# Sparse attention and a two-layer network on one core: GpSimd's casts of batch 1 ahead of its memsets, mask comparison and loads of batch 2

## The chip, the core and the metric

The kernel runs on one core of a Trainium2 chip. The core has five engines that run side by side, each through its own list of instructions in order: TensorE (PE; its weight loads are shown apart as PEld), VectorE (DVE), ScalarE (ACT), GpSimd (POOL) and SyncE (SP), which here only starts transfers. The metric is the device time of one execution in microseconds (us), as the median of several runs. An engine waits for another through semaphores, and a waiting instruction holds up everything behind it on its engine.

## What is computed

The reference first computes attention with two kinds of sparse mask, and then a two-layer network with a leaky activation on its output:

```python
scores = scale * np.matmul(q, k.transpose(0, 1, 3, 2))        # 8 batches, 8 heads, 576 positions, 64 wide
mask_local = (rel >= 0) & (rel < stride)                      # heads 0 to 3, stride 32
mask_strided = (rel >= 0) & (pos[None, :] % stride == pos[:, None] % stride)   # heads 4 to 7
scores = np.where(masks[None, :, :, :], scores, -1000000000.0)
attn = exp(scores - max) / (sum + 1e-09)
x = (attn @ v), heads side by side                            # 4608 rows of 512
h = x @ w_in                                                  # 512 to 2048
g = np.maximum(h, 0.0) + alpha * np.minimum(h, 0.0)
out = g @ w_out                                               # 2048 to 512
```

q, k, v and the weights arrive as float32; the kernel multiplies in float16.

## The kernel before, in words

A batch has four pairs of heads: pairs 0 and 1 of a batch are local (queries in blocks of 96), pairs 2 and 3 strided (blocks of 72). So pairs 4 to 7 are batch 1, and a "unit" is the local or the strided half of a batch: unit 2 is batch 1 local, unit 3 batch 1 strided, unit 4 batch 2 local. The network works on chunks of 512 rows, nine in all.

Each pair goes through the same steps. `load_qk` (L126) brings q and k in as float32 for the local halves (tiles `ql`, `kl`), the strided halves of later batches already as float16. `cast_l` (through `cast_copy`, L213 on ScalarE, L215 on VectorE, L217 on GpSimd) turns the local ones to float16. `transpose_piece` (L280) turns blocks of q and k on TensorE into PSUM, and ScalarE or VectorE copies them to `qT` and `kT`; `tails` does the same for the last 64 positions. `score_early` (L334) or `score_both` (L450) multiplies q and k, ScalarE takes the exponentials into one of six `et` tiles, and a multiplication by the 0/1 mask `mmul` follows, on VectorE (L355) in the early pairs and on GpSimd (L470, L477) later. `pv_piece` (L512) multiplies by v, in two or three groups of blocks; VectorE divides by the row sum (L521, L523). `x_piece` (L533) turns the result into `xT`, the input of the network. The transposes, the products with v and `x_piece` share three PSUM buffers, so a new one has to wait until an earlier one has been copied out.

A chunk's first layer is 16 pieces of four matmuls (`lin1_piece`, L678), each followed by ScalarE (`neg`, L697) and VectorE (`gT`, L700). The second layer of chunk 0 is 16 pieces of four matmuls (`lin2_piece`, L715); every fourth of a row block ends in a copy (L720) and a store (L721) from SyncE. Chunks from 1 on use a scheme with seven products in place of eight for 2 x 2 blocks, with sums of weights (`w_sums`, L748, VectorE) and of `gT` (`g_sum`, L760).

All instructions keep the order in which the program writes them (`keep`). The order around the change is written by hand as lists of tokens that `run` works off. List `first` (L949) does batch 0's attention. Then the rest of the weights and batch 1 are loaded from GpSimd (L968 to L970), the loop at L978 computes the first layer of chunk 0, and the list at L999 weaves batch 1's attention into chunk 0's second layer: `("M", i)` is a piece of the second layer, `("T", u, "q")` transposes of unit u, `("t", u)` its tails, `("C", 1, "q", 0, "pool")` the cast of one half of batch 1's local q on GpSimd, `("V", ...)` a copy of v, `("S", g)` the scores of pair g, `("K", g)` its masks, `("P", g, i)` group i of its product with v, `("X", g)` its `x_piece`, `("O", ...)` a copy of the overlap of v's blocks, and `("I", fn, ...)` any other call.

Before the change GpSimd does three things late in the first layer and early in the second (L984 to L987 and L1000 to L1004): it sets columns 640 to 800 of the six `et` tiles to zero (L986; VectorE sets 576 to 640 at the start, L912), it makes `mmul` by a comparison of the additive mask (L987), and it issues the loads of batch 2's local q and k (L126), tails (L187) and v (L205), partly ahead of the two casts of batch 1 (L217). A piece that is not part of attention of batch 1, the deferred exponentials, concerns later chunks: `score_both` puts some of its exponentials off (`defer`), and `pv_piece` (L488) runs those that it needs before it starts.

Of the kernel before, what the change touches and what calls it, by code (L numbers as in the profile page):

```python
# [11 lines left out]
ALU = mybir.AluOpType  # L12
# [20 lines left out]
def kernel(  # L33
# [10 lines left out]
    nc = tc.nc  # L44
    keep = tc.keep_in_program_order
# [27 lines left out]
    mmul = cpool.tile([128, 360], F16)  # L73
    madd = consts[:, 128:488]
# [27 lines left out]
    ets = [cpool.tile([128, 800], F16, name=f"et{i}") for i in range(NE)]  # L102
# [7 lines left out]
    def load_qk(b, strided, nm):  # L110

        h0 = 4 if strided else 0
        src = q if nm == "q" else k
        if strided and b:
            t16 = hpool.tile([128, 2, 512], F16, tag=f"{nm}s", bufs=2, name=f"{nm}s")
            cast16[(b, True, nm)] = t16
        else:
            t16 = hpool.tile([128, 2, 512], F32, tag=f"{nm}l", bufs=2, name=f"{nm}l")  # L120
            loaded[(b, strided, nm)] = t16
        base = src[b, h0 : h0 + 1, 0:1, :]
        eng = nc.sync if (b > 2 and not strided) or (b == 0 and strided) else nc.gpsimd
        if b == 0 and strided and nm == "q":
            eng = nc.scalar
        keep(eng.dma_start(t16, bass.AP(  # L126
            tensor=base.tensor, offset=base.offset,
            ap=[[8 * D, 64], [2 * S * D, 2], [S * D, 2], [1, 8 * D]])))
# [41 lines left out]
    def cast_l(b, nm, eng="pool", ts=(0, 8)):  # L170
        if (b, False, nm) not in cast16:
            cast16[(b, False, nm)] = hpool.tile(
                [128, 8, 2, 64], F16, tag=f"{nm}l16", bufs=2, name=f"{nm}l16")
        t16 = cast16[(b, False, nm)]
        src = loaded[(b, False, nm)].rearrange("p f (t d) -> p t f d", t=8)
        cast_copy(eng, t16[:, ts[0] : ts[1]], src[:, ts[0] : ts[1]])
# [42 lines left out]
    def cast_v(b, pr, eng):  # L219

        v16 = vss[b % 2]
        cast_copy(eng, v16[0:72, 2 * pr : 2 * pr + 2, :, 0:64],
                  loaded[b][0:72, 1024 * pr : 1024 * pr + 1024].rearrange(
                      "p (h t d) -> p h t d", h=2, t=8))
        cast16[(b, True, "v")] = v16
# [133 lines left out]
    def run_masks(P=None):  # L359

        for z in list(dmask):
            z[0] += P is None
            if z[0] > 1 or z[1] is P:
                z[2]()
                dmask.remove(z)
# [57 lines left out]
    defer, defer_et = [], {}  # L423
# [61 lines left out]

    def pv_piece(P, a):
        run_masks(P)
        while defer and any(P.et[z][0] is defer_et["et"] for z in P.et):  # L488
            defer.pop(0)()
        if P.x16 is None:  # L490
            if P.xd and P.strided:
                P.x16 = x16s
            else:
                P.x16 = xpool.tile([128, 1024], F16, tag="x16", name="x16")
        raw = P.strided and P.b == 0
        v16 = None if raw else cast16[(P.b, P.strided, "v")]
        grp = P.pgroups[a]
        r = 72 if P.strided else 128
        pv = pspool.tile([128, 512], F32, tag="ps", name="pv")
        nb = 2 * len(grp)  # L500
        for x in range(nb):
            t, hh = grp[x // 2], x % 2
            et, c = P.et[(t, hh)]
            if raw:
                d0 = 512 * (2 * P.pr + hh) + 64 * t
                for o, rhs in ((pv[:, 65 * x : 65 * x + 64], loaded[0][0:r, d0 : d0 + 64]),
                               (pv[:, 65 * x + 64 : 65 * x + 65], vss[0][0:r, 0, 0, 64:65])):
                    keep(nc.tensor.matmul(
                        o, et[0:r, c : c + 128], rhs, start=(x == 0 and o.shape[1] == 64),
                        stop=(x == nb - 1 and o.shape[1] == 1), skip_group_check=True))  # L510
                continue
            keep(nc.tensor.matmul(  # L512
                pv[:, 65 * x : 65 * x + 65], et[0:r, c : c + 128],
                v16[0:r, 2 * P.pr + hh, t, :] if P.strided else v16[:, 6 * (2 * P.pr + hh) + t, :],
                start=(x == 0), stop=(x == nb - 1), skip_group_check=True))
        while late:
            late.pop(0)()
        w = P.w
        rc = rpool.tile([128, 8], F32, tag="rc", name="rc")
        pvv = pv[0:w, 0 : 65 * nb].rearrange("r (c e) -> r c e", e=65)  # L520
        keep(nc.vector.reciprocal(rc[0:w, 0:nb], pvv[:, :, 64]))  # L521
        c0 = 128 * grp[0]
        keep(nc.vector.tensor_tensor(  # L523
            P.x16[0:w, c0 : c0 + 64 * nb].rearrange("r (c e) -> r c e", e=64),
            pvv[:, :, 0:64],
            rc[0:w, 0:nb].unsqueeze(2).to_broadcast([w, nb, 64]), op=ALU.mult))
# [16 lines left out]
    def x_dma(P):  # L543
        base = (P.b % 4) * S
        if P.strided:
            P.xs = xpool.tile([128, 8, 80], F16, tag="xs", bufs=2, name="xs")
            keep(nc.sync.dma_start_transpose(P.xs, P.x16[0:80, :]))
        else:
            keep(nc.sync.dma_start_transpose(
                xT[:, P.hp, base : base + S].rearrange("r (w p) -> r w p", p=96), P.x16[0:96, 0:768]))  # L550
# [26 lines left out]
    for g in range(7, npair + 2):  # L577
        c = g // 4
        a, p, t = g, g - 1, g + 1
# [28 lines left out]
        for i, (kind, fn) in enumerate(seq):  # L608
# [6 lines left out]
            def run(fn=fn, extra=extra, g=g, c=c, kind=kind, lastp=(i == lastP), first=(i == 0), i_last=(i == len(seq) - 1)):  # L615
                fn()
                for b, pr in extra:
                    if pr in ("q", "k"):
                        if b < LX:
                            cast_l(b, pr, "act" if b == 3 else "pool")  # L620
                        if b + 1 < LX:
                            load_qk(b + 1, False, pr)
                        continue
                    cast_v(b, pr, "pool")
                    if pr == 1 and b > 2 and b + 1 < B:
                        load_v(b + 1, True)
                if kind == "Tk" and g % 4 == 3 and c + 3 < LX:
                    load_tail(c + 3, False)
                if lastp:
                    if 4 * DX <= g - 1 < npair and pairs[g - 1].xd:  # L630
                        x_dma(pairs[g - 1])
                    if g % 4 == 3 and DX <= c + 1 < B:
                        transpose_d()
                    if g % 4 == 2 and DX <= c and c + 1 < B:
                        load_d(c + 1)
                    if g % 4 == 1 and DX < c and c + 1 < B:
                        load_v(c + 1, False)
                if first and g % 4 == 2 and LX <= c + 1 < B:
                    transpose_l(c + 1)
                if i_last and g % 4 == 3 and LX <= c + 2 < B:  # L640
                    for nm in "qk":
                        load_l(c + 2, nm)
                if first and 4 * DX <= g - 3 < npair and pairs[g - 3].xd and pairs[g - 3].strided:
                    x_copy(pairs[g - 3])
# [264 lines left out]
        keep(nc.vector.memset(kTs[i][:, :, 0:32], 0.0))  # L909
        keep(nc.vector.memset(kTs[i][:, :, 608:672], 0.0))  # L910
    for t in ets:
        keep(nc.vector.memset(t[:, 576:640], 0.0))  # L912
    load_tail(0, False)
    load_v(0, True)
    load_v(0, False)
# [13 lines left out]
    def w_next(*which):  # L929
        for z in which:  # L930
            load_w(*z)
# [33 lines left out]
                late.pop(0)()  # L965

    run(first)
    w_next((2, True), (3, True))  # L968
    load_unit(1, True)
    load_unit(1, False)  # L970
# [7 lines left out]
    for m in (2, 1, 0, *range(3, 16)):  # L978
        if m in (3, 4):
            banks.append(pspool.tile([128, 512], F32, tag="ps", name="hx"))  # L980
            turn.insert(0, m)
        lin1_piece(0, m)
        attn_n(0, 0)
        if m == 6:  # L984
            for t in ets:
                keep(nc.gpsimd.memset(t[:, 640:800], 0.0))  # L986
            keep(nc.gpsimd.tensor_scalar(mmul, madd, -1.0, 1.0, op0=ALU.is_ge, op1=ALU.mult))  # L987
    for z in (3, 4):
        turn.remove(z)
    do.update({  # L990
# [6 lines left out]
        "I": lambda fn, *a: fn(*a),  # L997
    })
    run([  # L999
        ("M", 0), ("M", 4), ("I", load_qk, 2, False, "q"), ("I", load_qk, 2, False, "k"),  # L1000
        ("C", 1, "q", 0, "pool"), ("I", w_sums, nc.vector, (1,)), ("M", 5), ("M", 6),
        ("I", load_tail, 2, False), ("M", 1), ("I", w_sums, nc.vector, (2,)), ("T", 3, "q"),
        ("M", 2), ("T", 3, "k"), ("I", w_sums, nc.vector, (4,)), ("V", 1, 0, "dve"),
        ("I", load_v, 2, False), ("t", 3), ("M", 7), ("C", 1, "k", 1, "pool"), ("M", 3),  # L1004
        ("V", 1, 1, "dve"), ("S", 6), ("M", 8), ("C", 1, "q", 1, "dve"), ("K", 6),
        ("C", 1, "k", 0, "dve"), ("T", 2, "q"), ("P", 6, 0), ("S", 7), ("P", 6, 1), ("M", 9),
        ("T", 2, "k"), ("t", 2), ("M", 10), ("K", 7), ("P", 6, 2), ("S", 5), ("P", 7, 0), ("M", 11),
# [68 lines left out]
```

## Time and profile before

| | before |
|---|---|
| three runs, us | 300.86, 299.57, 301.13 (median 300.86) |
| profiled execution | 300.0 us, span 298.1 us |
| TensorE clock granted | 1.00 |
| busy share VectorE, ScalarE, GpSimd | 76%, 58%, 57% |
| read from and written to memory | 38.60 MB, 9.44 MB |

The page gives for one execution the busy time of each engine, the span in slices, the transfers, the chain of work that ended last, and the costliest groups of instructions. In a row of the timeline the columns are start in us, duration in us, engine, line of the kernel, operation, tiles as output<-inputs, shape and count; in brackets stands how long the engine had been idle before it, and what released it. Matmuls are pipelined and their ends are modelled, so starts say more than ends. DMA-issuing instructions of GpSimd appear with the time that the issue took; the landing of a transfer is given apart.

### The profile page before, as it was taken

How to read it: one execution, taken by the hardware profiler on the slowest of the kernel's cores; microseconds unless marked ns; L12 is line 12 of the kernel's file. 1: busy time of each engine (PE TensorE's matmuls, PEld its weight loads, DVE VectorE, ACT ScalarE, POOL GpSimd, SP SyncE). 2: the span in 40 equal slices, each digit the busy share in tenths (PEclk: the TensorE clock that was granted, in tenths of full speed). 3: DMA queues.
4: the chain of work that ended last, by engine and by line, in shares of the span. 5: the costliest groups of instructions: out<-in, count | busy, mean ns of one | idle time of the engine just before them, and what ended most of it. 6: DMA issues, size and time to landing. Idle time of an engine off the chain costs nothing.

```text
span 298.1 us, 7107 instructions
## 1 busy us (share of the span) xinstructions
PE 289.9 (97%) x2808; PEld 193.6 (65%) x2808; DVE 227.8 (76%) x427; ACT 173.5 (58%) x325; POOL 168.5 (57%) x182
## 2 busy tenths in 40 slices
PE   7899998999999999999999999999999999999995
PEld 3664445644886478646898887468746864784584
DVE  5788868979975988488848894889488858946872
ACT  3566556888557773776377636763676257406620
POOL 8952289359757996777777778665555003101300
PEclk9999999999999999999999999999999999999999
DMA  7999999995998969999999999993811140022004
GB/s 219 204 202 207 205 238 266 170 175 178 177 154 186 111 100 127 173 192 160 132 209 177 138 141 182 184 144 54 201 22 21 24 141 0 2 71 73 0 2 141
DMA packets 102273, 41.01 MB, mean 138 GB/s; under 512 B 80720, under 2 KB 99424, under 8 KB 102240
## 3 DMA queue, kind: packets, MB, share of 16 engines
q0 software_dynamic: 56336, 19.25, 61.1%
q1 hardware_dynamic: 45632, 20.78, 35.3%
q10 hardware_dynamic: 272, 0.52, 0.6%
q8 instruction: 22, 0.36, 0.6%
q14 instruction: 11, 0.09, 0.1%
HBM read 38.60 MB, written 9.44 MB: 161 GB/s over the span
## 4 chain that ended last, share of the span: by engine, by line
PE 80%; DMA 11%; POOL 4%; issue 2%; DVE 2%; ACT 1%; POOLq 0%
PE hb L678 36%; PE hb L811 32%; DMA ks<-in_k_dram 6%; PE pv L512 4%; DMA win<-in_moe_w_in_dram 3%; PE sp L450 2%; DMA ql<-in_q_dram 2%; PE hb L715 2%; PE opl L811 1%; PE xp L533 1%; PE tp L280 1%; DVE gT L700 1%; PE sph L450 1%; POOL ql L217 1%; POOL vl L205 0%
## 5 line engine op out<-in xcount | busy, mean ns | idle before, releaser
L678 PE MATMUL hb<-xT,win 128*128 128x512 f16 (+1 forms) x616 | 127.2, 357 | 0.0
L700 DVE SCALAR_TENSOR_TENSOR gT<-neg,oma,hb 128x512 f16<-128x512 f32 x138 | 100.7, 744 | 33.0 <-ACT neg L697 26.3
L697 ACT ACTIVATE neg<-hb 128x512 f32<-128x512 f32 x138 | 82.1, 597 | 32.7 <-PE hb L678 31.5
L678 PEld LDWEIGHTS <-win 128*128 128x128 f16 x640 | 60.0, 98 | 53.8
L760 POOL TENSOR_TENSOR gsum<-gT 128x512 f16<-128x512 f16 x23 | 26.5, 1152 | 68.9 <-DVE gT L700 68.9
L811 PEld LDWEIGHTS <-gsum 128*128 128x128 f16 x512 | 47.3, 98 | 6.0 <-DVE gsum L760 0.5
L811 PEld LDWEIGHTS <-gT 128*128 128x128 f16 x384 | 35.9, 98 | 6.0 <-issue 0.5
L470 POOL TENSOR_TENSOR et<-et,mmul 128x576 f16<-128x576 f16 (+1 forms) x24 | 30.6, 1274 | 14.6 <-issue 7.8
L823 ACT COPY o<-hb 128x512 f32<-128x512 f32 (+1 forms) x32 | 18.1, 569 | 32.5 <-PE hb L811 32.5
L523 DVE TENSOR_TENSOR x<-pv,rc 96x384 f16<-96x384 f32 (+2 forms) x65 | 34.5, 531 | 2.2
L811 PE MATMUL hb<-wout,gT 128*128 128x256 f16 x248 | 30.8, 273 | 0.1
L811 PE MATMUL hb<-wout,gsum 128*128 128x256 f16 x248 | 30.5, 272 | 0.0
L811 PE MATMUL hb<-wsum,gsum 128*128 128x256 f16 x248 | 30.3, 273 | 0.0
L477 POOL TENSOR_TENSOR et<-et,mmul 72x576 f16<-72x576 f16 (+2 forms) x24 | 29.3, 1220 | 0.4 <-ACT et L474 0.4
L826 DVE TENSOR_TENSOR o<-hb,o 128x512 f32<-128x512 f32 (+1 forms) x24 | 16.3, 681 | 17.0 <-PE hb L811 12.5
L464 ACT ACTIVATE et<-sp 72x576 f16<-72x576 f32 (+2 forms) x24 | 16.4, 685 | 20.6 <-PE sph L450 17.2
L512 PEld LDWEIGHTS <-et 72*128 72x128 f16 (+1 forms) x416 | 21.9, 98 | 8.0 <-issue 1.3
L474 ACT ACTIVATE et<-sph 72x288 f16<-72x288 f32 (+2 forms) x48 | 17.8, 388 | 0.0
L521 DVE RECIPROCAL rc<-pv 72x6 f32<-72x6 f32 (+2 forms) x80 | 14.5, 181 | 2.9 <-PE pv L512 2.4
L715 PE MATMUL hb<-wout,gT 128*128 128x512 f16 x64 | 15.6, 379 | 0.2 <-ACT osb L720 0.2
L811 PE MATMUL hb<-wsum,gT 128*128 128x256 f16 x120 | 15.3, 273 | 0.0
L760 DVE TENSOR_TENSOR gsum<-gT 128x512 f16<-128x512 f16 (+2 forms) x17 | 14.7, 865 | 0.2
(117 smaller groups left out, 318.0 us busy)
## 6 DMA issues: line engine op xcount, KB each, us to landing
out_dram<-o SPq DMA_DIRECT2D x31, 256.0 KB, 3.1
stv<-in_v_dram POOLq DMA_DIRECT2D x8, 288.0 KB, 8.4
vl<-in_v_dram POOLq DMA_DIRECT2D x6, 384.0 KB, 9.3
wout<-in_moe_w_out_dram POOLq DMA_DIRECT2D x4, 512.0 KB, 16.9
qsd<-in_q_dram POOLq DMA_DIRECT2D x6, 288.0 KB, 7.6
ksd<-in_k_dram POOLq DMA_DIRECT2D x6, 288.0 KB, 7.1
kl<-in_k_dram SPq DMA_DIRECT2D x3, 512.0 KB, 5.1
ql<-in_q_dram POOLq DMA_DIRECT2D x3, 512.0 KB, 6.4
```

What stands on the lines that cost most here:

```text
L470: keep(nc.gpsimd.tensor_tensor(mv, mv, m, op=ALU.mult))
L474: keep(nc.scalar.activation(ev[:, n * y : n * y + n], sps[y][0:r, 0:n], AF.Exp, scale=SCALE))
L477: keep(nc.gpsimd.tensor_tensor(mv, mv, m, op=ALU.mult))
L512: keep(nc.tensor.matmul(pv[:, 65 * x : 65 * x + 65], et[0:r, c : c + 128], v16[0:r, 2 * P.pr + hh, t, :] if P.strided else v16[:, 6 * (2 * ...
L523: keep(nc.vector.tensor_tensor(P.x16[0:w, c0 : c0 + 64 * nb].rearrange("r (c e) -> r c e", e=64), pvv[:, :, 0:64], rc[0:w, 0:nb].unsqueeze ...
L678: keep(nc.tensor.matmul(hps[:, dst : dst + w], win16[:, kk, 128 * m : 128 * m + 128], xT[:, kk, src : src + w], start=(first and kk == kks ...
L697: keep(nc.scalar.activation(neg, hps, AF.Relu, scale=-1.0))
L700: keep(nc.vector.scalar_tensor_tensor(gTs[n][:, m, :], neg, oma[:, m : m + 1], hps, op0=ALU.mult, op1=ALU.add))
L715: keep(nc.tensor.matmul(ops, gTs[n][:, kf, 128 * mt : 128 * mt + 128], wout16[:, kf, :], start=(kf == 0), stop=(kf == 15)))
L760: keep(eng.tensor_tensor(o[:, k0:k1], x[:, k0:k1], y[:, k0:k1], op=op))
L811: keep(nc.tensor.matmul(dst, lhs[:, kf, 128 * mt : 128 * mt + 128], rhs[:, kf, :], start=(first and own and kf == 0), stop=(kf == 7), skip ...
L823: keep(nc.scalar.copy(o, x))
```

## The change

The change clears GpSimd's list ahead of the two casts of batch 1's local q and k:

- The zeros of columns 640 to 800 of `et` join VectorE's memsets at the start of the program.
- The comparison that makes `mmul` stays on GpSimd, but stands right after the list `first`, ahead of the last two loads of w_out.
- The loads of batch 2's local q and k go to SyncE (the rule `b > 2` becomes `b >= 2`) and stand after the piece `("M", 3)`; batch 2's tails and v stay on GpSimd and stand after the second cast.
- `pv_piece` runs deferred exponentials only if the group of blocks that it is about to multiply needs them, not if any of the pair does.

What is computed stays the same, and so does the number of transfers. On TensorE and ScalarE the order of the instructions is the same as before; on VectorE only the six memsets are larger.

```diff
-        eng = nc.sync if (b > 2 and not strided) or (b == 0 and strided) else nc.gpsimd
+        eng = nc.sync if (b >= 2 and not strided) or (b == 0 and strided) else nc.gpsimd
...
-        while defer and any(P.et[z][0] is defer_et["et"] for z in P.et):
+        while defer and any(P.et[t, y][0] is defer_et["et"] for t in P.pgroups[a] for y in range(2)):
...
-        keep(nc.vector.memset(t[:, 576:640], 0.0))
+        keep(nc.vector.memset(t[:, 576:800], 0.0))
...
     run(first)
+    keep(nc.gpsimd.tensor_scalar(mmul, madd, -1.0, 1.0, op0=ALU.is_ge, op1=ALU.mult))
     w_next((2, True), (3, True))
...
-        if m == 6:
-            for t in ets:
-                keep(nc.gpsimd.memset(t[:, 640:800], 0.0))
-            keep(nc.gpsimd.tensor_scalar(mmul, madd, -1.0, 1.0, op0=ALU.is_ge, op1=ALU.mult))
...
-        ("M", 0), ("M", 4), ("I", load_qk, 2, False, "q"), ("I", load_qk, 2, False, "k"),
-        ("C", 1, "q", 0, "pool"), ("I", w_sums, nc.vector, (1,)), ("M", 5), ("M", 6),
-        ("I", load_tail, 2, False), ("M", 1), ("I", w_sums, nc.vector, (2,)), ("T", 3, "q"),
+        ("M", 0), ("M", 4), ("C", 1, "q", 0, "pool"), ("I", w_sums, nc.vector, (1,)), ("M", 5), ("M", 6),
+        ("M", 1), ("I", w_sums, nc.vector, (2,)), ("T", 3, "q"),
         ("M", 2), ("T", 3, "k"), ("I", w_sums, nc.vector, (4,)), ("V", 1, 0, "dve"),
-        ("I", load_v, 2, False), ("t", 3), ("M", 7), ("C", 1, "k", 1, "pool"), ("M", 3),
+        ("t", 3), ("M", 7), ("C", 1, "k", 1, "pool"), ("I", load_tail, 2, False),
+        ("I", load_v, 2, False), ("M", 3), ("I", load_qk, 2, False, "q"), ("I", load_qk, 2, False, "k"),
         ("V", 1, 1, "dve"), ("S", 6), ("M", 8), ("C", 1, "q", 1, "dve"), ("K", 6),
```

## The prediction

> **What bounds the kernel now.** I read the page's busy shares and chain first, then busy time in stretches of ten microseconds, then the order of time on each engine around the one stretch where TensorE is not full.
>
> ```profile
> PE 289.9 (97%) x2808; PEld 193.6 (65%) x2808; DVE 227.8 (76%) x427; ACT 173.5 (58%) x325; POOL 168.5 (57%) x182
> PE 80%; DMA 11%; POOL 4%; issue 2%; DVE 2%; ACT 1%; POOLq 0%
> ```
>
> TensorE is the bound: 97% busy, 80% of the chain. GpSimd is only 57% busy, yet 4% of the chain (some 12 us) runs over it.
>
> ```profile
> 40.00:50.00 10.00, 8.24 (x97) 4.71 (x96) 7.62 (x18) 6.44 (x17) 9.83 (x17) 1.00 1.72 264
> 50.00:60.00 10.00, 10.00 (x142) 6.58 (x140) 9.50 (x27) 8.07 (x15) 5.11 (x8) 1.00 1.74 170
> ```
>
> The columns are the stretch, its length, and busy us of TensorE, its weight loads, VectorE, ScalarE and GpSimd. Between 20 and 290 us this is the only such stretch in which TensorE is idle for more than 0.1 us (1.76 us), and there GpSimd is full. The next stretch fills TensorE, with VectorE at 95%. TensorE's own order shows who it waits for:
>
> ```profile
> 43.88 1.02 PE L715 MATMUL hb<-wout,gT 128*128 128x512 f16 x4 [0.20 <-ACT osb L720]
> 45.61 0.62 PE L280 MATMUL tp<-consts,ql 128*128 128x128 f16 x8 [0.70 <-POOL ql L217]
> 47.77 0.39 PE L280 MATMUL tp<-consts,kl 128*128 128x128 f16 x4
> 48.90 0.40 PE L280 MATMUL tp<-consts,kl 128*128 128x128 f16 x4 [0.74 <-POOL kl L217]
> ```
>
> Both stops are casts of batch 1's local q and k on GpSimd. The ends are modelled, so I measure from start to start: four L715 matmuls take 0.87 us elsewhere, so the transposes could have begun at 44.75 (they did at 45.61: 0.86 us lost); four transposes take 0.22, so the second half could have begun at 47.99 (48.90: 0.91 us). Together 1.77 us. GpSimd's order says why the casts were late:
>
> ```profile
> 40.79 1.11 POOL L986 MEMSET et<- 128x160 f16 x6
> 42.01 1.47 POOL L987 TENSOR_SCALAR mmul<-consts 128x360 f16<-128x360 f16 x1
> 43.43 0.79 POOL L126 DMA_DIRECT2D ql<-in_q_dram  x1
> 44.21 0.72 POOL L126 DMA_DIRECT2D kl<-in_k_dram  x1
> 44.93 0.62 POOL L217 CAST ql<-ql 128x512 f16<-128x512 f32 x1
> 46.76 1.46 POOL L205 DMA_DIRECT2D vl<-in_v_dram  x1
> 48.20 0.65 POOL L217 CAST kl<-kl 128x512 f16<-128x512 f32 x1
> ```
>
> Nothing here is idle: 4.1 us of memsets, comparison and load issues stand ahead of the q cast, 2.8 us of issues ahead of the k cast.
>
> [...] a 512 KB load costs GpSimd 0.72 to 0.79 us of issue and SyncE 0.60 to 0.82. [...] of two equal copies of v, the one beside GpSimd's memsets took 0.75 us, the other, beside the comparison, 0.44 (rows below). [...] here 32 words take 85 ns, 256 take 272, that is 0.83 ns a word.
>
> **The change part by part.** *Memsets to VectorE.* Six of 32 words become six of 112: 6 x 80 x 0.83 ns = 0.40 us more, at 4.2 us. The next VectorE work (the q cast at 5.18) waits 0.64 us for its load, so this is hidden. Saved on GpSimd: 1.11 us at 40.8.
>
> *Comparison into layer 1.* 1.47 us of GpSimd move to about 17.9 us, ahead of two wout loads. Those are queued behind transfers that take 16 to 17 us to land, and the q load after them waited for an earlier transfer (0.42 us) anyway; so the DMA engines stay fed and landings do not move. Cost 0.
>
> *Loads of batch 2.* ql and kl leave GpSimd (1.51 us) for SyncE, after the second store, near 44.6 us. The tail and v issues (2.8 us) go behind the k cast. SyncE has nothing else queued until a store that is ready only at 52.5.
>
> *The casts.* They now follow the v issue that ends at 40.8, and wait for their data: the loads issued at 32.33 and 34.88 landed 9.9 and 9.6 us later, at 42.2 and 44.5. Cast q ends at 42.9, cast k at 45.2. TensorE wants them at 44.75 and, after moving up by 0.86, at about 47.1. Both waits go: 1.77 us. The new wait, k cast on its load, holds up the tail and v issues behind it until 45.2; they stood at 45.5 before, so nobody loses.
>
> *VectorE as the limiter.* From here it has to keep up:
>
> ```profile
> 41.43 0.75 DVE L215 COPY vs<-stv 72x1024 f16<-72x1024 f16 x1
> 42.36 0.44 DVE L215 COPY vs<-stv 72x1024 f16<-72x1024 f16 x1
> 44.47 1.41 DVE L355 TENSOR_TENSOR et<-et,mmul 72x576 f16<-72x576 f16 x2 [1.33 <-ACT et L342]
> 48.20 0.69 DVE L215 COPY kT<-tp 128x512 f16<-128x512 f16 x1 [0.27 <-PE tp L280]
> 49.45 0.22 DVE L215 COPY qT<-tt 128x128 f16<-128x128 f16 x1 [0.56 <-PE tt L304]
> 54.50 0.81 DVE L355 TENSOR_TENSOR et<-et,mmul 128x576 f16<-128x576 f16 x2
> ```
>
> If the slow copy becomes 0.44 us, the chain after it (q tails, k tails on ScalarE, the stores' copies, the bank that the matmuls at 43.88 waited for, the first masks) comes 0.31 earlier. VectorE's idle time before 50.4 is 0.27 + 0.56, and the first mask pair takes 1.41 us beside GpSimd's cast where later pairs take 0.81 to 0.90, say 0.5 more. So VectorE can come forward by 0.83 + 0.5 = 1.33 us, or 1.64 with the copy. After 50.4 it runs with no gap over 0.2 us until 58.3, and TensorE is tied to it there:
>
> ```profile
> 54.99 0.37 PEld L512 LDWEIGHTS <-et 128*128 128x128 f16 x6 [0.18 <-DVE et L355]
> ```
>
> So of TensorE's 1.77 (2.08 with the copy) between 1.33 and 1.64 passes. I take 1.5 us. After 59 us TensorE has no idle left in the view by stretches, so what is won there stays to the end. *The condition on deferred exponentials* leaves the order of every ScalarE, VectorE and TensorE instruction as it was: 0.
>
> Sum: 300.86 - 1.5 = 299.36, say 299.4 us.
>
> **The rivals.** *Everything passes* (0.10): VectorE's later pieces also shorten as GpSimd is quieter; 2.08 us, 298.8. For it: only 0.18 us of TensorE's weight loads wait for VectorE. Against: VectorE's 95%.
>
> *Batch 2's q lands late* (0.27): ScalarE casts it at 52.43, and TensorE's transposes at 53.64 wait for that; to win 1.5 us it must be there by 50.9. Issued by GpSimd at 43.43 and 44.21 the two loads took 6.4 and 7.4 us. Issued at 44.6 by SyncE, behind two stores of 256 KB, 7.4 us gives 52.0, and 0.4 us is left: 300.4. Against: SyncE's loads at 64 and 72 us landed in 4.6 to 5.1.
>
> *Batch 1's v lands late, slower* (0.13): SyncE's megabyte now runs beside v (landed at 47.9) instead of behind it. If all of it goes first, at some 200 GB/s, v comes 5 us later, at 52.9; GpSimd's copy (0.83), two issues (1.5) and second copy (0.81) end at 56.0, where the matmuls of pair 4 stood at 55.15 before: 0.9 us slower, 301.8. [...] Against: an even split takes less than half of that, and the copies have over 3 us in hand.
>
> **How the numbers follow.** Likeliest (0.50): a gain of 1.2 to 1.8 us, 299.4. The bound of 0.5% is 1.50 us, inside this case. The three runs of before reach from 299.57 to 301.13 and the profiled one is 300.0, so the median is rather high, and I put 0.37 of the 0.50 on faster. Faster 0.37 + 0.10 = 0.47; same 0.13 + 0.27 = 0.40; slower 0.13. The range leaves out the slower case and the best end of the first rival: 298.5 to 301.0.
>
> **What would show it.** Right: no GpSimd releaser on the L280 rows, casts ending near 42.9 and 45.2, TensorE reaching chunk 1 (12 matmuls of L678, at 58.89 before) near 57.4. VectorE's tie shows as weight loads waiting for its masks or evacuations between 50 and 57. Wrong: L280 on ql waiting for ScalarE's cast (late load), L512 on vl waiting for GpSimd's copy (late v), or a later start of the transposes at 39 us, if the moved comparison starved the DMA queue.

## The result, and the profile after

| | before | after |
|---|---|---|
| median of ten executions each, us | 299.76 (299.49 to 301.6) | 298.33 (297.81 to 298.81) |
| ratio of the means | | 0.9937, 95% interval 0.9919 to 0.9955 |
| span of the profiled execution, us | 298.1 | 296.6 |

The change saves 1.43 us by these medians, and 1.84 us by the means (300.15 and 298.31), by which the ratio goes, as all ratios below. In two later groups, each on one chip with its own executions of the kernel before, the medians differ by 1.57 us (ratio 0.9945, interval 0.9926 to 0.9964) and 1.48 us (0.9942, 0.992 to 0.9965). The prediction said 1.5 us less, but counted from 300.86 us, and so gave 299.4 with a range from 298.5: the measured 298.33 lies just below it. The same kernel's medians in the later groups, 298.6 and 298.84, lie inside that range, so the time alone is a weak test; the waits below are a better one.

The busy shares and the chain that ended last, on the page of the changed kernel:

```profile
PE 289.7 (98%) x2808; PEld 193.9 (65%) x2808; DVE 227.8 (77%) x427; ACT 173.7 (59%) x325; POOL 168.0 (57%) x174
...
PE 89%; DVE 4%; DMA 2%; ACT 2%; issue 1%; SPq 0%; ACTq 0%
```

GpSimd, 4% of the chain before, is gone from it, and transfers fell from 11% to 2%; all engines are as busy as before. The view by stretches (start and end, length, then busy us of TensorE, weight loads, VectorE, ScalarE, GpSimd) shows where:

```profile
40.00:50.00 10.00, 9.69 (x126) 5.88 (x125) 8.29 (x22) 7.92 (x20) 8.18 (x10) 1.00 1.74 255
50.00:60.00 10.00, 10.00 (x133) 6.26 (x131) 9.30 (x24) 8.26 (x15) 4.66 (x6) 1.00 1.68 180
```

TensorE is busy 9.69 us where it was 8.24: 1.45 us. In its timeline both waits for GpSimd are gone; only the wait for ScalarE's copy ahead of the matmuls of line 715 is left (0.31 us, 0.20 before):

```profile
43.72 1.02 PE L715 MATMUL hb<-wout,gT 128*128 128x512 f16 x4 [0.31 <-ACT osb L720]
44.58 0.61 PE L280 MATMUL tp<-consts,ql 128*128 128x128 f16 x8
...
46.73 0.61 PE L280 MATMUL tp<-consts,kl 128*128 128x128 f16 x8
...
57.09 1.24 PE L678 MATMUL hb<-xT,win 128*128 128x512 f16 x5
```

The transposes of k are one group of eight now (before: four, a stop of 0.74 us, four), and chunk 1 begins at 57.09 us in place of 58.89. GpSimd's timeline shows the casts waiting for nothing but their data, and the issues behind them:

```profile
41.93 1.35 POOL L217 CAST ql<-ql 128x512 f16<-128x512 f32 x1 [0.95 <-DMA ql<-in_q_dram]
43.74 0.61 POOL L217 CAST kl<-kl 128x512 f16<-128x512 f32 x1 [0.46 <-DMA kl<-in_k_dram]
44.29 0.64 POOL L187 DMA_DIRECT2D tl<-in_q_dram  x1
44.92 0.62 POOL L187 DMA_DIRECT2D tl<-in_k_dram  x1
45.77 1.44 POOL L205 DMA_DIRECT2D vl<-in_v_dram  x1 [0.23 <-PE hb L334]
```

Laying the two lists of TensorE's starts side by side gives how much earlier each instruction begins ("the lead" below):

| at (before) | 39 | 43.88, L715 | 45.61, ql | 48.90, kl | 49.13 to 110 | from 116 |
|---|---|---|---|---|---|---|
| lead, us | -0.03 | 0.16 | 1.03 | 1.94 | 1.82 to 1.79 | 1.45 |

The first wait is worth 1.03 - 0.16 = 0.87 us, the second 1.94 - 1.03 = 0.91 (predicted: 0.86 and 0.91). Two small losses follow: 0.12 at once, and 0.34 between 110 and 116 us, which the prediction had not foreseen. There VectorE adds up pieces of `gT` (L760). The timeline of before shows one of GpSimd's masks and VectorE's sums, that of after the sums alone:

```profile
108.79 1.28 POOL L477 TENSOR_TENSOR et<-et,mmul 72x576 f16<-72x576 f16 x1
...
109.13 1.24 DVE L760 TENSOR_TENSOR gsum<-gT 128x512 f16<-128x512 f16 x1
110.29 1.28 DVE L760 TENSOR_TENSOR gsum<-gsum,gT 128x1024 f16<-128x1024 f16 x2
```

```profile
107.34 0.52 DVE L760 TENSOR_TENSOR gsum<-gT 128x512 f16<-128x512 f16 x1
107.78 2.36 DVE L760 TENSOR_TENSOR gsum<-gsum,gT 128x1024 f16<-128x1024 f16 x2
```

Together 2.5 us before and 2.9 after: a different one of the sums is slow, before the single one beside the mask. GpSimd's timeline of the changed kernel has that mask beside the pair, from 107.53 to 108.99, and explains why it stands there now:

```profile
90.31 2.02 POOL L217 COPY vs<-stv 72x1024 f16<-72x1024 f16 x2 [4.01 <-DMA stv<-in_v_dram]
...
107.53 1.46 POOL L477 TENSOR_TENSOR et<-et,mmul 72x576 f16<-72x576 f16 x1
```

Before, these copies of batch 3's strided v began at 91.58, after 3.49 us of waiting. So TensorE and VectorE come 1.8 us earlier, GpSimd's list only 1.27, because it waits for a landing; VectorE and GpSimd meet in another phase. The pair ends at 110.14, 1.15 us after the mask (108.99), and takes 1.28 us where no mask is beside it, as in the timeline of before. In two later profiles where this mask and the pair meet (the loads alone, and the third of the changed kernel) it ends 1.15 and 1.16 us after the mask. So it ends as if nearly all of it were done behind the mask; that is an inference from these times. Behind the sums VectorE copies tails of q, and ScalarE's next copy waits for that one; in its timeline of after:

```profile
112.13 0.27 ACT L213 COPY kT<-tt 128x128 f16<-128x128 f16 x1 [1.79 <-DVE qT L215]
```

It stood at 113.56 before, so ScalarE is only 1.43 us ahead here, and TensorE, which goes on with ScalarE's results, falls back to a lead of 1.45.

### The profile page after: what moved, and what is told of

Read it like the earlier page. It is cut to its first block, busy times and chain, and to the rows that moved or that the text cites. A ratio compares the mean times of both kernels' runs of the same rounds, so it can differ in the third digit from the quotient of the medians.

```text
span 296.6 us, 7099 instructions
## 1 busy us (share of the span) xinstructions
PE 289.7 (98%) x2808; PEld 193.9 (65%) x2808; DVE 227.8 (77%) x427; ACT 173.7 (59%) x325; POOL 168.0 (57%) x174
## 4 chain that ended last, share of the span: by engine, by line
PE 89%; DVE 4%; DMA 2%; ACT 2%; issue 1%; SPq 0%; ACTq 0%
PE hb L678 38%; PE hb L811 30%; PE hb L715 5%; PE pv L512 4%; DMA kl<-in_k_dram 2%; PE sp L450 2%; PE hx L678 2%; PE tp L280 2%; PE xp L533 1%; DVE gT L700 1%; PE opl L811 1%; PE sph L450 1%; DVE gsum L760 1%; PE pv L508 1%; ACT neg L697 1%
## 5 line engine op out<-in xcount | busy, mean ns | idle before, releaser
L760 POOL TENSOR_TENSOR gsum<-gT 128x512 f16<-128x512 f16 x23 | 26.5, 1150 | 68.8 <-DVE gT L700 68.8
L715 PE MATMUL hb<-wout,gT 128*128 128x512 f16 x64 | 15.6, 379 | 0.3 <-ACT osb L720 0.3
L217 POOL COPY vs<-stv 72x1024 f16<-72x1024 f16 x12 | 12.1, 1031 | 4.0 <-DMA stv<-in_v_dram 4.0
```

The source lines that it names most:

```text
L715: keep(nc.tensor.matmul(ops, gTs[n][:, kf, 128 * mt : 128 * mt + 128], wout16[:, kf, :], start=(kf == 0), stop=(kf == 15)))
L760: keep(eng.tensor_tensor(o[:, k0:k1], x[:, k0:k1], y[:, k0:k1], op=op))
```

## The experiments

My theory after the comparison: the whole gain is the two waits at 45.6 and 48.9, it is bounded by VectorE right behind them, and a part is given back at 110 us by a collision that hangs on one landing. Rivals: the gain comes from the other moves (memsets and comparison); SyncE's issue of the loads is of no account; the loss at 110 us is chance.

**The memsets and the comparison alone.** The loads and issues stay in GpSimd's list.

```diff
-        keep(nc.vector.memset(t[:, 576:640], 0.0))
+        keep(nc.vector.memset(t[:, 576:800], 0.0))
...
     run(first)
+    keep(nc.gpsimd.tensor_scalar(mmul, madd, -1.0, 1.0, op0=ALU.is_ge, op1=ALU.mult))
...
-        if m == 6:
-            for t in ets:
-                keep(nc.gpsimd.memset(t[:, 640:800], 0.0))
-            keep(nc.gpsimd.tensor_scalar(mmul, madd, -1.0, 1.0, op0=ALU.is_ge, op1=ALU.mult))
```

> The kernel before, with only the memsets moved to VectorE and the comparison moved into layer 1; batch 2's loads stay on GpSimd ahead of the casts. Theory A (the queue ahead of the casts is what counts, and either half of the change shortens it enough): q's cast can start when its data are there, near 42.3 us, k's ends near 47.0, about when TensorE wants it; both waits of TensorE on GpSimd go, TensorE is 1.6 to 1.9 us ahead of before at 50 us, span about 296.5 to 296.8. Theory B (both halves are needed): k's cast is still late by 0.5 us or more, TensorE is 1.0 to 1.3 us ahead, span near 297.0.

Measured: 300.96 us (298.64 to 303.7, 20 executions) against 300.06 for the kernel before: ratio 1.0025, interval 1.0004 to 1.0047. The spread was new, so the same kernel was run once more later, to see where it comes from:

> The kernel before with the memsets and the comparison moved and the loads left in place, once more, to see what spreads its times from 298.6 to 303.7 us. Theory: in part of the executions something lands late and TensorE stands for over 2 us, after which it runs at about half its clock for some 4 us; a profile over 301 us shows such a gap and a stretch with a granted clock near 0.5, and a profile under 300 us shows none. Rival: no stall over 1 us in any profile, and the slower executions lose in many small pieces.

Measured: 299.3 us (298.41 to 301.19, 18 executions) against 300.32: ratio 0.9965, interval 0.9944 to 0.9987. TensorE's and GpSimd's timelines of that second profile:

```profile
48.59 0.40 PE L280 MATMUL tp<-consts,kl 128*128 128x128 f16 x4 [1.73 <-POOL kl L217]
```

```profile
43.62 0.64 POOL L187 DMA_DIRECT2D tl<-in_k_dram  x1
46.46 1.45 POOL L205 DMA_DIRECT2D vl<-in_v_dram  x1 [2.20 <-PE pv L512]
47.90 0.63 POOL L217 CAST kl<-kl 128x512 f16<-128x512 f32 x1
```

The two groups differ by more than their intervals, so the times do not settle what this half is worth. The profiles show that it removes the wait for the q cast (the lead jumps by 0.87 and 0.86 us at the q transposes in the two profiles) but not the one for the k cast. That one stands behind the issue of batch 2's v, and the issue itself waits: 0.82 us in the first profile, 2.20 in this one, so TensorE waits 0.35 and 1.73 us. The theory expected such a stop, of over 2 us, only in executions over 301 us, the rival none over 1 us; here an execution of 299.78 us had one of 1.73, so neither holds. Those of the first group between 302.0 and 302.9 us had mean granted clocks of 0.992 to 0.994, those under 300.7 us 0.997 to 1.000, which fits a longer stop followed by a stretch at a lower clock, as two profiles below have it behind stops of 3.42 and 2.61 us (0.50 to 0.66 for 4 us, mean of the execution 0.994); no such execution of this kernel was profiled, so that remains an inference. What the v issue waits for is not shown. The trace names a matmul each time, and not the same one; in both profiles the issue begins 0.01 to 0.02 us after batch 1's tails of k have landed (45.08 and 46.44 us), the sixth load before it on GpSimd. No run varies that.

**The loads and the order alone.** Memsets and comparison stay where they were.

```diff
-        eng = nc.sync if (b > 2 and not strided) or (b == 0 and strided) else nc.gpsimd
+        eng = nc.sync if (b >= 2 and not strided) or (b == 0 and strided) else nc.gpsimd
...
-        ("M", 0), ("M", 4), ("I", load_qk, 2, False, "q"), ("I", load_qk, 2, False, "k"),
-        ("C", 1, "q", 0, "pool"), ("I", w_sums, nc.vector, (1,)), ("M", 5), ("M", 6),
-        ("I", load_tail, 2, False), ("M", 1), ("I", w_sums, nc.vector, (2,)), ("T", 3, "q"),
+        ("M", 0), ("M", 4), ("C", 1, "q", 0, "pool"), ("I", w_sums, nc.vector, (1,)), ("M", 5), ("M", 6),
+        ("M", 1), ("I", w_sums, nc.vector, (2,)), ("T", 3, "q"),
...
-        ("I", load_v, 2, False), ("t", 3), ("M", 7), ("C", 1, "k", 1, "pool"), ("M", 3),
+        ("t", 3), ("M", 7), ("C", 1, "k", 1, "pool"), ("I", load_tail, 2, False),
+        ("I", load_v, 2, False), ("M", 3), ("I", load_qk, 2, False, "q"), ("I", load_qk, 2, False, "k"),
```

> The kernel before, with only the order of casts and loads changed (q and k of batch 2 to SyncE, tails and v after the second cast); memsets and comparison stay on GpSimd ahead of the casts. Theory A: 2.6 us still stand ahead of q's cast, which ends near 44.1, before TensorE's 44.6; k's near 45.2; both waits go, and only the 0.16 us that came from the quick copy of v is missing: TensorE 1.6 to 1.7 us ahead at 50 us, the copy of v at 41.4 still takes 0.75 us. Theory B: q's cast is late, TensorE 1 us ahead or less.

Measured: 298.14 us (297.51 to 298.57, four executions) against 300.06: ratio 0.993, interval 0.9913 to 0.9947. Theory A holds: TensorE is 2.07 us ahead at 50 us, 0.24 of it from before 39 us. This half alone reaches what the whole change reaches, and with the old condition on deferred exponentials. GpSimd's timeline says why the rest adds nothing:

```profile
41.12 2.04 POOL L987 TENSOR_SCALAR mmul<-consts 128x360 f16<-128x360 f16 x1
43.13 0.60 POOL L217 CAST ql<-ql 128x512 f16<-128x512 f32 x1
45.01 0.96 POOL L217 CAST kl<-kl 128x512 f16<-128x512 f32 x1 [1.27 <-DMA kl<-in_k_dram]
```

With memsets and comparison still ahead, the q cast ends at 43.73, and TensorE begins its transposes at 44.47 in this profile.

**Only the q and k loads to SyncE.** The tails' and v's issues stay ahead of the k cast.

```diff
-        eng = nc.sync if (b > 2 and not strided) or (b == 0 and strided) else nc.gpsimd
+        eng = nc.sync if (b >= 2 and not strided) or (b == 0 and strided) else nc.gpsimd
...
-        ("M", 0), ("M", 4), ("I", load_qk, 2, False, "q"), ("I", load_qk, 2, False, "k"),
+        ("M", 0), ("M", 4),
...
+        ("I", load_qk, 2, False, "q"), ("I", load_qk, 2, False, "k"),
         ("V", 1, 1, "dve"), ("S", 6), ("M", 8), ("C", 1, "q", 1, "dve"), ("K", 6),
```

> The kernel before, with only batch 2's q and k loads moved to SyncE, at the changed kernel's place between the second and third store; memsets, comparison, and the tail and v issues ahead of the k cast stay. Theory, that the 1.5 us of these two issues was what stood in excess ahead of both casts: the q cast starts near 43.5 and ends at 44.1, before TensorE's 44.75; the k cast starts near 46.7 and ends at 47.3 against 47.1 wanted, so all but 0.1 to 0.2 us of the 1.77 is won: 1.5 us less than before with the later loss of 0.3, the same as with the whole change within 0.2 us. Rival: the order of tail and v issues counts too, because the v issue waits for an earlier transfer and holds the k cast until 47.9 or later; then only 0.9 to 1.1 us is won by 50 us, and about 0.8 at the end.

Measured: 298.91 us (298.05 to 300.01) against 300.17: ratio 0.9957, interval 0.9945 to 0.9969; the changed kernel in the same group 298.6. The timeline of GpSimd:

```profile
43.67 0.60 POOL L217 CAST ql<-ql 128x512 f16<-128x512 f32 x1
...
45.52 1.55 POOL L205 DMA_DIRECT2D vl<-in_v_dram  x1
47.06 0.62 POOL L217 CAST kl<-kl 128x512 f16<-128x512 f32 x1
```

This profile is of the slowest of the 22 executions (300.01 us), but the two steps can be read from it: the lead goes from -0.23 (L715) to 0.63 (ql) and 1.16 (kl), 0.86 for the first wait and 0.53 of the second one's 0.91. So the 1.5 us of issues account for most of it, and the v issue ahead of the k cast still costs TensorE 0.4 us, even where it waits for nothing; of the two theories each holds for one cast.

**Batch 2's loads at their new place, but issued by GpSimd.**

```diff
-        eng = nc.sync if (b >= 2 and not strided) or (b == 0 and strided) else nc.gpsimd
+        eng = nc.sync if (b > 2 and not strided) or (b == 0 and strided) else nc.gpsimd
```

> The changed kernel, with batch 2's local q and k issued by GpSimd instead of SyncE at the same place of the program. They would be issued near 47.2 and 48.0 us, behind v's issue, and land after 6.4 to 7.4 us, at 53.6 and 55.4. If the landing of batch 2's q decides what VectorE, ScalarE and TensorE do after 50 us, ScalarE's cast, at 50.6 in the changed kernel, waits until 53.6 and TensorE's transposes of q, at 51.8, until 54.8: some 3 us lost, span 298.5 to 299.6. If the place of the issue does not matter, span 296.6.

Measured: 304.04 us (303.31 to 306.2, four executions) against 300.06: ratio 1.014, interval 1.0097 to 1.0184. Timelines of ScalarE and TensorE, then the view by stretches (the granted clock stands behind the five engines, 1.00 being full):

```profile
54.54 1.04 ACT L213 CAST ql<-ql 128x1024 f16<-128x1024 f32 x1 [3.59 <-DMA ql<-in_q_dram]
```

```profile
55.64 0.62 PE L280 MATMUL tp<-consts,ql 128*128 128x128 f16 x8 [3.42 <-ACT ql L213]
```

```profile
56.00:58.00 2.00, 2.00 (x22) 1.17 (x20) 1.57 (x4) 2.00 (x5) 0.00 (x0) 0.66 1.23 219
58.00:60.00 2.00, 2.00 (x14) 0.90 (x12) 0.74 (x2) 0.58 (x1) 0.00 (x0) 0.50 1.41 190
```

GpSimd reaches the two issues at 48.02 and 48.73, behind v; on SyncE they go out at 44.15 and 44.95. The q load lands too late, which is the mechanism of the rival "batch 2's q lands late", with a wait of 3.42 us, about the 3 us expected; the clock of 0.66 and 0.50 behind it, which was not expected, costs a further 1.6 us of lead. So the move to SyncE is no mere relief of GpSimd: the later place in the list is affordable only with it.

**Batch 3's second strided v copied by ScalarE**, to take GpSimd off the landing.

```diff
-                    cast_v(b, pr, "pool")
+                    cast_v(b, pr, "act" if (b, pr) == (3, 1) else "pool")
```

> The changed kernel, with the second copy of batch 3's v on ScalarE instead of GpSimd. Theory: of the 1.82 us won by 50 us, 0.35 is lost near 112 us, because GpSimd, held up by the landing of that v, comes there only 1.3 us earlier than before while VectorE comes 1.8 earlier, so that VectorE's sums of gT meet GpSimd's mask of et in another phase and take 2.36 us in place of 1.28. With GpSimd 1 us ahead the sums should meet it less: the pair of sums near 107.8 takes about 1.3 us, and TensorE keeps 1.6 to 1.8 us, span 296.2 to 296.4. Rival: the loss at 112 us comes from TensorE's or ScalarE's own order there, and stays: span 296.6 or more.

Measured: 302.14 us (299.9 to 305.02) against 300.06: ratio 1.006, interval 1.0036 to 1.0084. The expectation failed. ScalarE's and TensorE's timelines and the stretches:

```profile
89.15 1.05 ACT L213 COPY vs<-stv 72x1024 f16<-72x1024 f16 x1 [4.46 <-DMA stv<-in_v_dram]
```

```profile
91.09 0.42 PE L533 MATMUL xp<-consts,x 72*128 72x72 f16 x8 [2.61 <-ACT et L474]
```

```profile
92.00:94.00 2.00, 2.00 (x9) 0.85 (x7) 0.00 (x0) 0.85 (x3) 2.00 (x3) 0.61 0.79 89
94.00:96.00 2.00, 2.00 (x6) 0.72 (x5) 0.75 (x1) 0.83 (x2) 2.00 (x3) 0.53 0.93 203
```

The edit moved the wait for the landing, not the landing: 4.46 us on ScalarE, with exponentials queued behind, and TensorE stood 2.61 us. It shows the landing of this v as a real limit near 90 us, which GpSimd had been absorbing.

**The landing itself earlier.** Two places for the issue of batch 3's strided v. First, six steps earlier, ahead of its local v, q and k:

```diff
                 if n == 1 and i == 14:
+                    load_v(3, True)
                     load_v(3, False)
...
-                if n == 1 and i == 20:
-                    load_v(3, True)
```

> The changed kernel, with batch 3's strided v loaded six steps earlier (just ahead of its local v instead of at step 20 of chunk 1). Theory, that GpSimd's train is anchored by the landing of that load: the load lands some 10 us earlier, GpSimd's two v copies no longer wait 4.0 us at 86.3 to 90.3, its masks run earlier, and VectorE's sums of gT (line 760) near 107 take 1.3 us as a pair instead of 2.36. TensorE keeps its 1.8 us past 114 us: about 0.3 to 0.4 us less than the changed kernel, 298.0 us by the clock of the ten runs. Rival 1: the bytes on the queue are the same and only their order changes, so batch 3's strided q and k land 2 to 3 us later, the transposes of them at 86 to 90 come late, and TensorE loses 0.5 to 3 us: 298.8 to 301. Rival 2: GpSimd only meets VectorE elsewhere, no difference over 0.2 us.

Measured: 298.42 us (297.5 to 301.93) against 300.17, beside 298.6 for the changed kernel: no difference that can be told. The profiled execution, one of the slower ones (299.51 us), shows in VectorE's and TensorE's timelines that there theory and rival 1 both came true:

```profile
109.01 0.42 DVE L760 TENSOR_TENSOR gsum<-gT 128x512 f16<-128x512 f16 x1
109.35 1.28 DVE L760 TENSOR_TENSOR gsum<-gsum,gT 128x1024 f16<-128x1024 f16 x2
```

```profile
96.19 0.30 PE L450 MATMUL sp<-qT,kT 64*128 64x72 f16 x8 [1.04 <-DMA kT<-ksd]
```

The collision is gone (1.7 us for the three sums), but the strided k, now behind the v, is late by 1.04 us. Second, right behind the strided k, so that no transfer changes places:

```diff
-                if n == 1 and i == 20:
+                if n == 1 and i == 17:
                     load_v(3, True)
```

> The changed kernel, with batch 3's strided v issued right behind batch 3's strided k (step 17 of chunk 1 instead of step 20): the same order of transfers, only the issue stands ahead of two masks on GpSimd instead of behind them, near 75.7 instead of 80.7 us. Theory, that the landing of this load anchors GpSimd's train, which after the change runs further behind VectorE's: it lands up to 5 us earlier, the wait of 3.6 to 4.0 us ahead of GpSimd's copies at 90.1 to 90.3 goes to under 1 us, VectorE's three sums (line 760) near 107 take 0.4 + 1.3 us instead of up to 0.5 + 2.4, and nothing lands later because nothing changes places: 0.1 to 0.4 us less than the changed kernel in the same group. Rival 1: [...] the load lands when it landed before and nothing moves (within 0.1). Rival 2: the earlier megabyte takes bandwidth from batch 3's strided k, TensorE waits for its transpose near 94 to 96 us as it did with the load six steps earlier (1.04 us): 0.5 to 1 us more.

> The changed kernel, for comparison on the same chip as the two others of this group. Theory: 1.4 to 1.6 us less than the kernel before, with TensorE 1.5 to 1.8 us earlier from 54 us on, and at most 0.4 us of that given back at 107 to 114 us. Rival: what it wins differs between chips by more than 0.5 us.

Measured: 298.42 us (297.5 to 299.99, span 295.7) against 300.32, ratio 0.992 (0.9888 to 0.9952); the changed kernel beside it 298.84 (297.43 to 299.76). GpSimd's and VectorE's timelines of the edited kernel:

```profile
75.36 0.71 POOL L197 DMA_DIRECT2D stv<-in_v_dram  x1
...
88.31 2.02 POOL L217 COPY vs<-stv 72x1024 f16<-72x1024 f16 x2 [2.33 <-DMA stv<-in_v_dram]
```

```profile
107.02 0.43 DVE L760 TENSOR_TENSOR gsum<-gT 128x512 f16<-128x512 f16 x1
107.36 1.29 DVE L760 TENSOR_TENSOR gsum<-gsum,gT 128x1024 f16<-128x1024 f16 x2
```

The issue moved by 5.3 us, the landing by only 1.8 to 2.0, so the wait fell from 3.8 to 4.0 us to 2.33 rather than to under 1. That is enough in this profile, which is of the fastest of its ten executions: the sums take 1.7 us, no transpose is late, and the lead of TensorE (2.07 at kl, 2.28 from 111 us) is kept to the end. The medians differ by 0.42 us, the means by 0.19 with a spread (standard deviation) of 0.7 in each: the profile shows the loss gone, but the times alone cannot tell this version from the changed kernel.

**The changed kernel again**, in the group of the early v:

> The changed kernel once more, on the same chip as the other kernels of this group. Theory: 1.4 us (0.48 per cent) less than the kernel before, between 1.2 and 1.9; TensorE's starts are 1.8 us earlier up to 110 us and 1.5 us earlier from 114 us on, with the pair of sums at 107 us over 2 us again. Rival: the loss at 110 us was chance of one profiled run, and the shift stays at 1.8.

Measured: 298.6 us (297.71 to 299.5) against 300.17. Three profiles of the same kernel now show what varies from one execution to the next:

| profile of the changed kernel | lead at 39 | at L715 | at kl | at 54.09 | loss from 110 to 116 | sums at 107 us |
|---|---|---|---|---|---|---|
| first | -0.03 | 0.16 | 1.94 | 1.80 | 0.34 | 0.52 + 2.36 |
| second, in the group of the v six steps earlier | -0.10 | 0.09 | 1.87 | 1.56 | 0.09 | 1.32 + 1.28 |
| third, in the group of the v behind k | 0.52 | 0.71 | 2.49 | 1.81 | 0.25 | 0.43 + 2.37 |

All leads are counted against the one profile of the kernel before. The two casts give 1.78 us in each. By 54 us 0.14, 0.31 and 0.68 us of it are gone again; the third had been 0.52 us ahead before the casts and is no further ahead than the first behind them. The third profile shows best that it is VectorE that takes this back, in the timelines of TensorE and of VectorE:

```profile
47.04 0.27 PE L304 MATMUL tt<-consts,tl 128*128 128x128 f16 x2 [0.24 <-DVE x L523]
```

```profile
46.34 0.55 DVE L523 TENSOR_TENSOR x<-pv,rc 72x384 f16<-72x384 f32 x1
46.81 0.68 DVE L215 COPY kT<-tp 128x512 f16<-128x512 f16 x1
47.41 0.21 DVE L215 COPY qT<-tt 128x128 f16<-128x128 f16 x1
47.54 1.35 DVE L355 TENSOR_TENSOR et<-et,mmul 72x576 f16<-72x576 f16 x2
```

The tails' transposes need a buffer that VectorE has yet to empty, VectorE runs without a gap, and the mask pair took 1.35 us here, 1.18 in the second profile, 1.00 in the first and 0.82 in the kernel before. The rest is the same kind of meeting as at 107 us: GpSimd's copy of batch 1's v (L217) has moved forward, from 48.91 us to between 47.38 and 47.63, and so stands beside the pair. In all three profiles the first mask ends 0.31 to 0.32 us after this copy does (48.52 and 48.21 us in the third).

The collision at 107 us follows the phase: kernels with both the single sum and the pair slow lost about 1 us of lead there (memsets and comparison alone, first profile: 1.28 + 2.36 and 1.10 us; loads alone: 1.08 + 2.36 and 0.90; q and k loads only: 1.27 + 2.36 and 1.10), those with the pair alone slow 0.25 to 0.34, the second profile, with the single sum alone slow as before, 0.09; where all were quick, 0.18 was won. So the expected slow pair came back in the third profile and not in the second, and the rival was right in part: how much is lost differs between executions of one kernel. What decides it is where GpSimd's list stands against VectorE's, and moving the landing moved that.

## Why the prediction was wrong, by its steps

**The starting point: wrong.** "Sum: 300.86 - 1.5 = 299.36" took the median of three executions as the base. Ten gave 299.76, and three later groups of 33 to 36 gave 300.06, 300.17 and 300.32: the base was 0.5 to 1.1 us too high. From 299.76 the same sum gives 298.26 against 298.33 measured. The text saw it ("the median is rather high": the profiled execution took 300.0) and used it only for the chances of faster and same; the number and the range were counted from the high base all the same. That is the step that failed; the gain itself, 1.5 us, was measured as 1.43, 1.57 and 1.48 by medians.

**The two waits: right.** 1.77 us predicted, 0.87 + 0.91 measured. Casts were to end near 42.9 and 45.2; they ended at 43.28 and 44.35. The q cast took 1.35 us instead of 0.62, beside VectorE's copies, and had over a microsecond to spare.

**Memsets, comparison, deferred exponentials at nothing: right as far as shown.** The lead at 39 us is -0.10 to 0.52 in the three profiles, and 0.24 in the run that leaves memsets and comparison in their places, so it differs between executions without them. Neither need have moved for the gain, as that run shows; it also keeps the old condition on deferred exponentials.

**The slow copy of v: half right.** It took 0.42 in place of 0.75 us, but TensorE got 0.19 of the 0.31. Its matmuls at 43.72 wait for the second of two copies by ScalarE (L720), which began at 43.09, right behind the modelled end (43.05) of the matmuls of line 715 ahead of it: there TensorE seems to limit itself. That GpSimd's memsets were what slowed the copy is not borne out: with the loads alone it took 0.71 us beside the comparison, after the memsets had ended.

**VectorE as the limiter: right in kind, uneven in size.** It was to let 1.33 to 1.64 us pass. Counted from L715 on, 1.64, 1.47 and 1.10 us passed in the three profiles by 54 us; counted from the start, 1.80, 1.56 and 1.81, two of them more than the upper figure.

**"What is won there stays to the end": wrong, by 0.1 to 0.3 us.** TensorE had no idle in the view by stretches, but VectorE's and GpSimd's relative phase changed, and sums at 107 us grew. That the lead ends at 1.45 to 1.55 us, close to the 1.5 predicted, is partly luck: VectorE let more pass than was counted on, and this loss, put at nothing, took it back. A view of idle times of before cannot show a collision that only the shifted kernel has; a list of what GpSimd waits for (the landing, 3.49 us) could have warned that it wouldn't come forward along.

**The rivals.** "Batch 2's q lands late" did not happen: from SyncE it took 5.4 us and landed at 49.54, before ScalarE took it up at 50.60; the same loads from GpSimd at that place made it happen at once. "Batch 1's v lands late" did not happen: GpSimd's copy waited 0.18 us for it and started at 47.39 (48.91 before). "Everything passes" (298.8 from the high base, 2.08 us) did not either.

## What to carry to other kernels

Count a gain from a base of as many executions as the result will have, and put the base's own uncertainty into the range: here the base alone was off by 0.5 to 1.1 us, for a gain of 1.5. When an engine's list holds a cast that TensorE waits for, first move away the issues ahead of it that may themselves wait (the v issue here: up to 2.20 us), and check that what is issued later still lands in time from the new engine. After any shift, look for engines that are held by a landing rather than by TensorE: they don't come along, and pairs of VectorE and GpSimd instructions meet anew (here two sums took 2.36 us in place of 1.28).

## What the hardware showed that I had not expected

- After stops of 3.42 and 2.61 us TensorE resumed at 55.64 and 91.09 us with the clock at 1.00, and lost it only then: the granted clock was 0.66 and 0.50 from 56 to 58 and 58 to 60 us in the one profile, 0.61 and 0.53 from 92 to 94 and 94 to 96 us in the other, and 0.98 and 1.00 in the next two microseconds. The mean over each of these executions was 0.994. After the stop of 1.73 us (memsets and comparison alone, second profile) it stayed at 1.00. What decides this is not shown by three stops.
- An issue of a load on GpSimd can hold its list. In the profiles of the kernel before and of the changed kernel no more than eight of GpSimd's loads are under way at once, and between 19 and 40 us eight of its issues in the one and seven in the other begin 0.28 to 0.29 us after the eighth load before them has landed; GpSimd stood idle for up to 2.03 us ahead of them. The v issue near 46 us stood still for at most 0.23 us in seven profiles and for 0.82 and 2.20 us in two, with fewer loads under way (six with its own); what it waits for there stays open.
- Moving an issue 5.3 us earlier moved the landing by 1.8 to 2.0 us.
